# Weight tiles converted in pairs inside their load slots, with the order of the work tuned anew, in a delta-rule attention followed by two MLPs

## The chip, the cores and the metric

One core of a Trainium2 chip runs the whole program. The metric is the device time of one execution in microseconds (us), lower is better; where several runs are shown, their median counts.

## The reference

Four batches of eight heads go through a delta-rule recurrence over 768 tokens with head dimension 48, and its output, laid out as 3072 tokens by 384, goes through two MLPs without norms:

```python
k_n = k / (norm(k, axis=-1) + 1e-6)
for t in range(S):
    y[:, :, t] = einsum('bhd,bhde->bhe', q[:, :, t], state)
    v_old = einsum('bhde,bhd->bhe', state, kt)
    state = state + bt * einsum('bhd,bhe->bhde', kt, vt - v_old)
x = y.transpose(0, 2, 1, 3).reshape(3072, 384)
h = x @ w_in;   g = h * sigmoid(1.702 * h);   x = g @ w_out        # 384 -> 2048 -> 384
h = max(x @ moe2_w_in, 0);   out = (h * h) @ moe2_w_out
```

## The kernel before, in words

**Attention.** The 768 tokens are 12 chunks of 64. All 32 heads lie side by side, 16 pairs of them. For each chunk `run_a` makes the products k·k and k·q on TensorE (PE), `solve_in`, `solve_norm` and `solve_prep` make a triangular system out of them, `solve_loop` solves it by 31 steps of two small instructions each (chunks 0 and 1 by `solve_blocks`, 15 steps on half-size blocks, closed by `merge`), and the scan (`scale_v`, `run_x`, `finish`, `run_w`, `run_v`, `run_y`, `run_s`) makes the output y and the next state. The solves of chunks 2 to 11 run on GpSimd (POOL); that of chunk 1 goes where `TUNE["solve1"]` says, VectorE (DVE) here; that of chunk 0 is on DVE.

**MLPs.** A unit (`step`) is one tile of 128 hidden features for one group of tokens: 9 matmuls of the first layer into a PSUM bank `h`, an activation (ScalarE, ACT), and, two units later, 9 matmuls of the second layer (`layer2`) into three banks `z` that collect over all 16 tiles. Each product is three matmuls, of a high part and a low part of both sides (hi·hi, lo·hi, hi·lo). A group is 512 tokens, two chunks, with 16 units; there are six groups per MLP. The first group is cut: 8 units on the 256 tokens of chunk 0, 8 units on those of chunk 1, then 8 units on all 512, so units 0 to 23; the second group begins with unit 24 and needs the outputs of chunks 2 and 3. While group j is computed, the two chunks of group j + 1 are solved and scanned.

**Weights.** They arrive as 64-bit floats, 384 of them per partition and tile (384 KB). There are 64 tiles, 32 for each MLP (`wi`, `wo`; then `vi` and `wo` again). `load_w` (L375) loads one tile into one of three slots `raw`; `split_w` (L380) converts it with five instructions: on ACT the high word scaled into the buffer `c0`, on ACT (or DVE, in the second MLP, `tail`) the top three bits of the low word into one of two buffers `c1`, on DVE the two joined by shift and or into `c1` (L349), on ACT the high part `hi`, on DVE or POOL the low part `lo` = joined − hi (L342). The slot is free once the third instruction has run; `c1` is free after the fifth. `convert` (L1044) does that for n tiles and issues the next load after each. The z results of the first MLP go out through the same slots.

**Order.** Nothing is in program order: `Program.flush` is a list scheduler. It keeps one ready queue for each engine, takes the operation with the lowest rank that its cost figures say is ready, and writes the instructions of each engine in that order, which the chip then keeps. Rank is the place in the Python program, so the `TUNE` tables (L31) set it: `first` and `conv` say after which unit how many tiles are converted, `scan`, `solve`, `gscan`, `gsolve` at which unit each part of a chunk's scan and solve stands, `spread` does so for the weights of the second MLP, `holds` and `late` hold back loads behind a tiny DMA, `norm_pool` names the chunks whose norms go on POOL, `v_pool` and `lo_both` what may go on POOL or DVE, `p_late` when the k·q products are taken out of PSUM. `warm`, `burst`, `tiny`, `lead`, `fills`, `pad` and `auto` put idle matmuls on zeros (L306, L680, L1058, `tiny` L1061) between the real ones, which keep PE busy in the early part. Operations marked `urgent` go ahead of their rank (the solve of chunk 0 and, with `solve1='dve'`, that of chunk 1).

Of the kernel before, what the change touches and what calls it, by code (L numbers as in the profile page):

```python
# [19 lines left out]
C = 64  # L20
# [12 lines left out]
    warm=(0, 1, 0, 2, 0, 1, 1, 0, 1, 0, 1, 0, 0, 0, 1, 0),  # L33
    burst=(2, 7, 120),
    spread=1.85,
# [3 lines left out]
    slack=0.1,  # L39
# [20 lines left out]
    gscan=(0.0, 2.0, 2.0, 3.5, 3.5, 7.5),  # L60
    gsolve=(-9.0, -8.0, -2.5, -1.5),
    solve={2: (-8.0, -7.0, -5.5, -2.5), 3: (3.0, 8.0, 12.0, 12.5), 4: (14.5, 19.0, 21.0, 21.5), 5: (21.5, 24.1, 30.2, 31.5)},
# [164 lines left out]
def kernel(  # L227
# [54 lines left out]
    s_sb = att.tile([128, NP, D], F32, name="s_sb")  # L282
# [3 lines left out]
    q_sb = several(att, "q", 2, [128, NP, C])  # L286
# [5 lines left out]
    kT_sb = att.tile([128, 4, 4, C], F32, name="kT_sb")  # L292
# [81 lines left out]

    def load_w(src, f):  # L375
        s = n_conv[0] % NR
        n_conv[0] += 1
        dma(raw_sb[s], src[:, f].rearrange("p (n two) -> p n two", two=2), [], [("raw", s)], 128, 8 * DM)

    def split_w(key, f, hi, lo):  # L380
        s, t = n_conv[1] % NR, n_conv[1] % 2
        n_conv[1] += 1
        raw, c0, c1 = raw_sb[s], c0_sb[0], c1_sb[t]
        low = raw.rearrange("p n two -> p (n two)").bitcast(U16).rearrange("p (n q) -> p n q", q=4)[:, :, 1]
        both = [("c1", t)]
# [36 lines left out]
    V = [("v", g, k) for g in range(2) for k in range(2)]  # L422

# [548 lines left out]
    zs_of = [(("raw", i), t.rearrange("p n two -> p (n two)").bitcast(F32)[:, :TT]) for i, t in enumerate(raw_sb)]  # L972

    def layer2(ph, j, f, c0, n, hi, lo, K):
# [8 lines left out]
        if f == NF - 1:  # L983
            dst = zd if ph == 1 else out
            for e in range(KX):
                key, zs = zs_of[ns[1] % NR]
# [54 lines left out]
    w1 = [x for f in range(NF) for x in ((w1_in, "wi", f, wi_hi, wi_lo), (w1_out, "wo", f, wo_hi, wo_lo))]  # L1041
    w1_load = list(w1)

    def convert(todo, load, n, key=None):  # L1044
        for _ in range(n):
# [3 lines left out]
            if load:  # L1049
                load_w(*(load[0][0], load.pop(0)[2]))  # L1050

    with tc.manual_schedule():
# [66 lines left out]
        convert([], w1_load, NR)  # L1119
# [27 lines left out]
        convert(w1, w1_load, TUNE["first"])  # L1147
# [75 lines left out]
        zs_of[:] = [(("zs", i), t) for i, t in enumerate(several(p2, "zs", NR, [128, TT]))]  # L1223
# [8 lines left out]
        w2 = [x for f in range(NF) for x in ((w2_in, "vi", f, vi_hi, vi_lo), (w2_out, "wo", f, wo_hi, wo_lo))]  # L1232
# [125 lines left out]
```

## Time and profile before

| | us |
|---|---|
| three runs | 971.37, 973.64, 976.02 (median 973.64) |
| the profiled execution | 970.17 |
| its span, first to last instruction | 968.4 |
| start of the units 0, 8, 16, 24 (first `h` matmul in the timeline) | 45.0, 94.2, 114.1, 167.2 |
| chunk 1, 2, 3 solved (transpose `Td<-U`) | 47.6, 114.6, 149.1 |

The profiled execution lies 3.5 us under the median. The span is what the trace shows; the other 1.8 us of the execution lie around it.

### The profile page before, as it was taken

How to read it: one execution, taken by the hardware profiler on the slowest of the kernel's cores; microseconds unless marked ns; L12 is line 12 of the kernel's file. 1: busy time of each engine (PE TensorE's matmuls, PEld its weight loads, DVE VectorE, ACT ScalarE, POOL GpSimd, SP SyncE). 2: the span in 40 equal slices, each digit the busy share in tenths (PEclk: the TensorE clock that was granted, in tenths of full speed). 3: DMA queues.
4: the chain of work that ended last, by engine and by line, in shares of the span. 5: the costliest groups of instructions: out<-in, count | busy, mean ns of one | idle time of the engine just before them, and what ended most of it. 6: DMA issues, size and time to landing. Idle time of an engine off the chain costs nothing.

```text
span 968.4 us, 25919 instructions
## 1 busy us (share of the span) xinstructions
PE 937.9 (97%) x11079; PEld 758.8 (78%) x11079; DVE 474.9 (49%) x943; ACT 455.0 (47%) x927; POOL 328.0 (34%) x700
## 2 busy tenths in 40 slices
PE   7788999999999999999999999999999999999998
PEld 4566877787687778778888888888888888888886
DVE  7767866724643672554325456643433433433332
ACT  5368786325624534452466465642332422422322
POOL 3158883885578388477700010000000000000000
PEclk9789999999999999999999999999999999999999
DMA  5466562304401330430025353220010100000000
GB/s 189 162 198 215 158 183 77 109 1 127 148 14 43 125 120 2 127 101 17 23 90 165 96 177 98 66 66 1 24 42 0 61 5 1 34 1 0 33 1 33
DMA packets 34633, 75.83 MB, mean 78 GB/s; under 512 B 6326, under 2 KB 7382, under 8 KB 34518
## 3 DMA queue, kind: packets, MB, share of 16 engines
q1 hardware_dynamic: 34518, 74.17, 24.6%
q8 instruction: 87, 1.43, 0.6%
q14 instruction: 28, 0.23, 0.1%
HBM read 63.64 MB, written 9.44 MB: 75 GB/s over the span
## 4 chain that ended last, share of the span: by engine, by line
PE 82%; DVE 5%; POOL 5%; ACT 3%; issue 3%; DMA 1%; SPq 0%; ACTq 0%; POOLq 0%; DVEq 0%
PE h L369 37%; PE z L369 36%; PE a L369 8%; POOL U L749 2%; POOL tmpp L745 2%; DMA xf_sb<-Td 1%; PE z L306 1%; DVE c L349 1%; ACT w_sb L331 1%; DVE glo L342 0%; DVE wo_lo L342 0%; DMA k_sb<-in_kt 0%; SPq L313 0%; ACT h L326 0%; ACT wi_hi L326 0%
## 5 line engine op out<-in xcount | busy, mean ns | idle before, releaser
L369 PE MATMUL z<-ghi,wo_hi 128*128 128x512 f32 (+1 forms) x600 | 231.4, 386 | 0.0
L369 PE MATMUL z<-glo,wo_hi 128*128 128x512 f32 (+1 forms) x600 | 229.6, 383 | 0.4 <-DVE glo L342 0.4
L369 PE MATMUL z<-ghi,wo_lo 128*128 128x512 f32 (+1 forms) x600 | 229.1, 382 | 0.0
L342 DVE TENSOR_TENSOR glo<-h,ghi 128x512 fp32r<-128x512 f32 (+1 forms) x200 | 133.4, 668 | 193.9 <-ACT ghi L326 192.8
L745 POOL TENSOR_TENSOR tmpp<-U,gu 128x126 f32<-128x126 f32 (+22 forms) x310 | 139.3, 449 | 60.9 <-DVE U L346 38.3
L342 DVE TENSOR_TENSOR h<-g_sb,h 128x512 f32<-128x512 f32 x96 | 66.8, 696 | 175.2 <-ACT g_sb L326 175.2
L326 ACT ACTIVATE ghi<-h 128x512 fp32r<-128x512 f32 (+1 forms) x200 | 115.7, 580 | 59.5 <-DVE h L342 56.2
L326 ACT ACTIVATE g_sb<-h 128x512 f32<-128x512 f32 x96 | 57.2, 596 | 173.4 <-PE h L369 172.6
L749 POOL TENSOR_TENSOR U<-U,tmpp 128x126 f32<-128x126 f32 (+22 forms) x310 | 129.8, 419 | 24.3
L369 PEld LDWEIGHTS z<-ghi,wo_hi 128*128 128x128 f32 x600 | 113.1, 189 | 23.5
L369 PEld LDWEIGHTS z<-glo,wo_hi 128*128 128x128 f32 x600 | 113.2, 189 | 23.1 <-DVE glo L342 1.1
L369 PEld LDWEIGHTS z<-ghi,wo_lo 128*128 128x128 f32 x600 | 113.2, 189 | 22.2 <-DVE wo_lo L342 0.2
L369 PE MATMUL h<-x_hi,wi_hi 128*128 128x512 f32 (+1 forms) x312 | 124.0, 398 | 4.2 <-DVE glo L342 3.2
L326 ACT ACTIVATE h<-h 128x512 f32<-128x512 f32 (+1 forms) x104 | 57.2, 551 | 145.2 <-PE h L369 144.8
L369 PE MATMUL h<-x_lo,wi_hi 128*128 128x512 f32 (+1 forms) x312 | 117.3, 376 | 1.4 <-issue 1.4
L369 PE MATMUL h<-x_hi,wi_lo 128*128 128x512 f32 (+1 forms) x312 | 117.2, 375 | 1.5 <-POOL wi_lo L342 0.8
L369 PE MATMUL h<-x_hi,vi_hi 128*128 128x512 f32 x288 | 112.0, 389 | 0.0
L369 PE MATMUL h<-x_hi,vi_lo 128*128 128x512 f32 x288 | 112.0, 389 | 0.0
L369 PEld LDWEIGHTS h<-x_hi,wi_hi 128*128 128x128 f32 x312 | 59.0, 189 | 20.0 <-DVE glo L342 4.9
L369 PEld LDWEIGHTS h<-x_hi,wi_lo 128*128 128x128 f32 x312 | 59.0, 189 | 13.8 <-issue 1.6
L369 PEld LDWEIGHTS h<-x_lo,wi_hi 128*128 128x128 f32 x312 | 59.1, 189 | 9.0 <-DVE x_lo L342 0.4
L369 PEld LDWEIGHTS h<-x_hi,vi_hi 128*128 128x128 f32 x288 | 54.0, 188 | 11.2
(153 smaller groups left out, 1156.9 us busy)
## 6 DMA issues: line engine op xcount, KB each, us to landing
raw<-in_w_in SPq DMA_DIRECT2D x32, 384.0 KB, 3.2
raw<-in_w_out SPq DMA_DIRECT2D x32, 384.0 KB, 3.9
kq<-in_kf SPq DMA_DIRECT2D x44, 256.0 KB, 3.5
kT_sb<-in_kq SPq DMA_DIRECT2D x11, 512.0 KB
q<-in_kq SPq DMA_DIRECT2D x11, 512.0 KB, 5.6
k_sb<-in_kt SPq DMA_DIRECT2D x12, 384.0 KB, 3.8
v_sb<-in_vt SPq DMA_DIRECT2D x12, 384.0 KB, 7.2
xf_sb<-zd SPq DMA_DIRECT2D x18, 256.0 KB, 3.1
```

What stands on the lines that cost most here:

```text
L306: e.matmul(out=z_ps[KX - 1][:, 0:w], lhsT=z0[:, 0:128], rhs=z0[:, 0:w], start=not z_open[0], stop=not z_open[0])
L326: pg.add("act", c_act(n, kw["out"].shape[0]), lambda e: e.activation(**kw), reads, writes, early)
L331: e.activation(out=out, in_=in_, func=AF.Copy)
L342: pg.add(queue, cost, lambda e: e.tensor_tensor(out=out, in0=in0, in1=in1, op=op), reads, writes, early)
L349: pg.add("dve", c_dve(n), lambda e: e.scalar_tensor_tensor(**kw), reads, writes, early)
L369: e.matmul(out=out, lhsT=lhsT, rhs=rhs, start=start, stop=stop)
L745: e.tensor_tensor(out=t, in0=U[:, c0 + lo:c0 + hi, w:w + 1].to_broadcast(shape), in1=gu[:, :w, w:w + 1].rearrange("p i o -> p o i").to_bro ...
L749: e.tensor_tensor(out=y, in0=y, in1=t, op=ALU.add)
```

## The change

A slot now holds two neighbouring tiles (768 KB), and there are two slots. All five instructions work on 768 elements instead of 384 and inside the slot: the high word is scaled in place, the top bits are written over the low word, the join is written over the high word, and `hi` and `lo` are made from there. `c0` and `c1` are gone. The slot is therefore free only after the fifth instruction. There is one conversion for each pair, 16 in each MLP, and `first`, `conv` and `spread` count pairs. The z results use thirds of the two slots. `tail` is on ACT in both MLPs. The code can also take spare buffers as slots (`extra`), but `NX = 0`. For that, two attention tiles are allocated as parts of larger ones, at the same size.

In the order of the work: the solve of chunk 1 goes to POOL and is no longer urgent; the norms of chunk 4 go to POOL; `scale_v` of chunk 2 may go to POOL; the loads of chunk 0's q stand behind those for chunk 1 (`q_first`); the first weight loads are no longer held behind the tiny DMA (`holds`); three pairs instead of three tiles are converted before unit 0 (`first`); the products k·q leave PSUM earlier (`p_late`); positions of scans and solves move by up to some units; and the idle matmuls are placed anew.

```diff
-    warm=(0, 1, 0, 2, 0, 1, 1, 0, 1, 0, 1, 0, 0, 0, 1, 0),
-    burst=(2, 7, 120),
-    spread=1.85,
+    warm=(0, 3, 0, 2, 3, 1, 0, 0, 1, 0, 1, 1, 3, 0, 3, 3),
+    burst=(0, 8, 80),
+    spread=1.0,
...
-    q_first=1,
+    q_first=0,
-    lead=0,
-    holds=(1, 1, 1),
-    late=8,
-    conv=(3, 1, 1, 4, 0, 1, 2, 0, 1, 0, 0, 0, 0, 3, 3, 1, 1, 4, 4, 1, 2, 1, 3, 0, 0, 4, 1, 1, 7, 0, 6, 6),
-    lo_both=99,
-    v_pool=2,
-    tiny=(0, 40),
+    lead=16,
+    holds=(1, 0, 1),
+    late=9,
+    conv=(0, 2, 0, 1, 1, 0, 0, 3, 0, 0, 0, 1, 0, 1, 3, 1, 1, 0, 0, 1, 0, 0, 1, 0, 3, 0, 0, 0, 0, 3, 1, 0),
+    lo_both=32,
+    v_pool=3,
+    tiny=(24, 224),
-    solve1='dve',
-    pad={27: 2, 147: 3, 36: 4, 33: 6, 217: 1, 48: 2, 28: 3, 20: 1, 41: 1, 12: 3},
-    auto=(3.0, 1.3, 290),
-    fills=(2, 0, 0, 0),
-    norm_pool=(1, 2),
-    tail=('act', 'both'),
+    solve1='pool',
...
+    auto=(4.5, 0.9, 110),
+    fills=(1, 0, 1, 13),
+    norm_pool=(1, 2, 4),
+    tail=('act', 'act'),
-    p_late=400,
-    scan={1: (-4.5, -4.5, -3.0, -2.5, -1.0, 1.0), 2: (11.5, 11.5, 11.5, 11.5, 12.5, 14.5), 3: (14.5, 19.0, 19.5, 19.5, 21.5, 22.0)},
+    p_late=50,
+    scan={1: (-9.5, -9.0, -8.0, -7.5, -4.5, -1.0), 2: (10.0, 11.0, 11.0, 13.0, 13.0, 15.0), 3: (17.5, 20.0, 20.0, 22.5, 22.5, 23.0)},
-    solve={2: (-8.0, -7.0, -5.5, -2.5), 3: (3.0, 8.0, 12.0, 12.5), 4: (14.5, 19.0, 21.0, 21.5), 5: (21.5, 24.1, 30.2, 31.5)},
+    solve={2: (-14.5, -10.5, -10.5, -6.0), 3: (7.0, 8.5, 12.5, 12.5), 4: (13.5, 19.0, 20.5, 21.5), 5: (23.0, 23.6, 29.7, 31.5)},
...
-    NR = 3
-    raw_sb = several(main, "raw", NR, [128, DM, 2], I32)
-    c0_sb = several(main, "c0", 1, [128, DM])
-    c1_sb = several(main, "c1", 2, [128, DM])
+    NR, PW = 2, 2
+    raw_sb = several(main, "raw", NR, [128, PW * DM, 2], I32)
...
     def split_w(key, f, hi, lo):
-        s, t = n_conv[1] % NR, n_conv[1] % 2
+        raw, K, (high, least_) = raw_of(n_conv[1])
         n_conv[1] += 1
-        raw, c0, c1 = raw_sb[s], c0_sb[0], c1_sb[t]
+        high, least_, n = [high], [least_], PW * DM
...
+        whole = raw[:, :, 1].bitcast(F32)
+        parts = whole.rearrange("p (f n) -> p f n", f=PW)
+        hi, lo = hi[:, f:f + PW, :], lo[:, f:f + PW, :]
...
-        act(DM, [("raw", s)], ["c0"], out=c0, in_=raw[:, :, 1].bitcast(F32), func=AF.Prelu, scale=2.0**-112, alpha=2.0**32)
...
-        pg.add(queue, cost, tail, [("raw", s)], both)
-        stt(DM, ["c0"] + both, both, out=c1.bitcast(I32), in0=c0.bitcast(I32), scalar=3, in1=c1.bitcast(I32),
+        act(n, K + high, high, out=whole, in_=whole, func=AF.Prelu, scale=2.0**-112, alpha=2.0**32)
...
+        pg.add(queue, cost, tail, K + least_, least_)
+        stt(n, K + high + least_, high, out=raw[:, :, 1], in0=raw[:, :, 1], scalar=3, in1=raw[:, :, 0],
             op0=ALU.logical_shift_left, op1=ALU.bitwise_or)
-        act(DM, both, [(key, f, 0)], out=hi[:, f, :], in_=c1)
-        tt(DM, both + [(key, f, 0)], [(key, f, 1)], lo[:, f, :], c1, hi[:, f, :], ALU.subtract,
-           ("pool", "dve") if n_conv[1] <= TUNE["lo_both"] else "pool")
+        act(n, K + high, H, out=hi, in_=parts)
+        tt(n, K + high + H, L, lo, parts, hi, ALU.subtract, ("pool", "dve") if n_conv[1] <= TUNE["lo_both"] else "pool")
...
-            if load:
-                load_w(*(load[0][0], load.pop(0)[2]))
+            if load and n_conv[0] < NR + max(n_conv[1], NX):
+                load_w(load[0][0], load.pop(0)[2])
```

## Rows read from the trace of the kernel before

**Rows 1.** The page: busy time of each engine.
```profile
PE 937.9 (97%) x11079; PEld 758.8 (78%) x11079; DVE 474.9 (49%) x943; ACT 455.0 (47%) x927; POOL 328.0 (34%) x700
```

**Rows 2.** Busy time by stage; the row "core 0" names the columns.
```profile
core 0: us, PE busy (x) PEld busy (x) DVE busy (x) ACT busy (x) POOL busy (x), PEclk, DMA share, GB/s
27.00:45.00 18.00, 14.49 (x365) 9.71 (x365) 11.59 (x62) 4.94 (x14) 0.00 (x0) 0.66 0.50 171
45.00:69.00 24.00, 20.19 (x653) 16.74 (x647) 17.51 (x37) 15.41 (x39) 12.77 (x26) 0.86 0.67 201
69.00:94.00 25.00, 19.80 (x472) 16.36 (x471) 16.95 (x29) 21.21 (x54) 19.92 (x40) 1.00 0.60 192
...
149.00:167.00 18.00, 17.48 (x555) 13.77 (x553) 11.42 (x29) 11.59 (x27) 4.33 (x10) 1.00 0.25 69
...
508.00:640.00 132.00, 132.00 (x584) 109.32 (x583) 74.37 (x134) 78.33 (x155) 7.51 (x7) 1.00 0.40 117
```

**Rows 3.** The chain of waits, pieces in order of time: start, length, what.
```profile
149.10 1.10 DVE Td L759
...
167.22 1.92 PE h L369 x7
...
254.25 2.81 DMA xf_sb<-Td
```

**Rows 4.** Timeline of POOL: start, length, line, operation, out<-in, count, [idle before].
```profile
45.35 1.48 POOL L342 TENSOR_TENSOR w_sb<-v_sb,nt 128x768 f32<-128x768 f32 x1 [19.11 <-PE a L369]
...
52.27 2.35 POOL L543 TENSOR_SCALAR_AFFINE_SELECT p<-p 64x1024 f32<-64x1024 f32 x2 [1.06 <-ACT p L331]
54.70 0.24 POOL L564 TENSOR_SCALAR sm_y<-gu 128x32 int32<-128x32 int32 x1
...
62.49 0.25 POOL L568 TENSOR_TENSOR sm_a<-sm_b,sm_nu 128x32 f32<-128x32 f32 x1
...
69.40 0.49 POOL L745 TENSOR_TENSOR tmpp<-U,gu 128x31 f32<-128x31 f32 x1 [0.59 <-DVE U L346]
```

**Rows 5.** Groups by shape: count, then busy us, mean ns, idle before.
```profile
L326 ACT ACTIVATE ghi<-h 128x512 fp32r<-128x512 f32 x184 | 109.8, 598 | 59.3 <-DVE h L342 56.2
...
L349 DVE SCALAR_TENSOR_TENSOR c<-c,c 128x384 int32<-128x384 int32 x64 | 39.4, 615 | 4.2 <-ACT c L326 3.6 <-ACT c L389 0.3
...
L326 ACT ACTIVATE wo_hi<-c 128x384 fp32r<-128x384 f32 x32 | 16.8, 524 | 8.6 <-DVE c L349 7.8
```

**Rows 6.** Instructions on the tile wi_lo: min/median/max ns, first and last start.
```profile
L342 DVE TENSOR_TENSOR wi_lo<-c,wi_hi x11: 543/559/848, 61.0 to 144.9; 128x384 fp32r<-128x384 f32 x11
...
L342 POOL TENSOR_TENSOR wi_lo<-c,wi_hi x5: 992/1005/1020, 22.9 to 140.0; 128x384 fp32r<-128x384 f32 x5
```

**Rows 7.** Timeline of ACT: conversions, first and last G of chunk 2.
```profile
46.85 0.39 ACT L331 ACTIVATE G<-a 128x256 f32<-128x256 f32 x1 [0.27 <-PE a L369]
...
48.19 0.54 ACT L326 ACTIVATE c<-raw 128x384 f32<-128x384 f32 x1
...
51.52 0.40 ACT L331 ACTIVATE G<-a 128x256 f32<-128x256 f32 x1
...
82.82 0.56 ACT L326 ACTIVATE c<-raw 128x384 f32<-128x384 f32 x1
```

**Rows 8.** Timeline of DVE: chunk 1's solve, first and last; chunk 2's system; one `lo`.
```profile
28.14 0.67 DVE L705 SCALAR_TENSOR_TENSOR U<-gu,U 128x15 f32<-128x15 f32 x4
...
45.10 0.29 DVE L708 TENSOR_TENSOR gu<-U,gu 128x14 f32<-128x14 f32 x2
45.31 1.55 DVE L710 TENSOR_TENSOR U<-U,gu 128x14 f32<-128x14 f32 x2
...
66.72 1.23 DVE L342 TENSOR_TENSOR gu<-gu,sm_s 128x1024 f32<-128x1024 f32 x1
...
88.02 0.85 DVE L342 TENSOR_TENSOR wi_lo<-c,wi_hi 128x384 fp32r<-128x384 f32 x1
```

**Rows 9.** The page: one load of a weight tile, KB and median us to landing.
```profile
raw<-in_w_in SPq DMA_DIRECT2D x32, 384.0 KB, 3.2
```

More of the change, by code (lines that the diff above doesn't have):

```diff
@@ L281 @@
     w_sb = att.tile([128, NP, D], F32, name="w_sb")
-    s_sb = att.tile([128, NP, D], F32, name="s_sb")
+    ks_sb = att.tile([128, 16 * C + NP * D], F32, name="ks_sb")
+    kT_sb = ks_sb[:, 0:16 * C].rearrange("p (g a t) -> p g a t", g=4, a=4)
+    s_sb = ks_sb[:, 16 * C:].rearrange("p (a d) -> p a d", d=D)
     kq1_sb = several(att, "kq1", 2, [128, 2, 4, C])
@@ L285 @@
     p_sb = several(att, "p", 2, [128, NP, C])
-    q_sb = several(att, "q", 2, [128, NP, C])
+    q2 = att.tile([128, 2, NP, C], F32, name="q2")
+    q_sb = [q2[:, i] for i in range(2)]
     G_sb = several(att, "G", 2, [128, NP, C])
@@ L373, with raw_of @@
     n_conv = [0, 0]
+    def raw_of(n):
+        own = [("half", n % (NX + NR), i) for i in range(2)]
+        if n < NX:
+            t, keys = extra[n]
+            return t.bitcast(I32).rearrange("p (m two) -> p m two", two=2), keys, own
+        s = (n - NX) % NR
+        return raw_sb[s], [("raw", s, i) for i in range(3)], own
     def load_w(src, f):
-        s = n_conv[0] % NR
+        raw, keys, own = raw_of(n_conv[0])
         n_conv[0] += 1
-        dma(raw_sb[s], src[:, f].rearrange("p (n two) -> p n two", two=2), [], [("raw", s)], 128, 8 * DM)
+        dma(raw, src[:, f:f + PW].rearrange("p f (n two) -> p (f n) two", two=2), [], keys + own, 128, 8 * DM * PW)
@@ L387, in tail @@
+        hi, lo = hi[:, f:f + PW, :], lo[:, f:f + PW, :]
+        H, L = ([(key, f + i, x) for i in range(PW)] for x in range(2))
         def tail(e):
             if e is nc.scalar:
-                e.activation(out=c1.bitcast(I32), in_=low, func=AF.Copy, scale=7.499 / 65535)
+                e.activation(out=raw[:, :, 0], in_=low, func=AF.Copy, scale=7.499 / 65535)
             else:
-                e.tensor_scalar(out=c1.bitcast(I32), in0=raw[:, :, 0], scalar1=29, scalar2=None, op0=ALU.logical_shift_right)
@@ L393, in split_w @@
-        act(DM, [("raw", s)], ["c0"], out=c0, in_=raw[:, :, 1].bitcast(F32), func=AF.Prelu, scale=2.0**-112, alpha=2.0**32)
-        queue, cost = {"dve": ("dve", 0.38), "act": ("act", 0.42), "both": (("dve", "act"), (0.38, 0.42))}[TUNE["tail"][n_conv[1] > 32]]
-        pg.add(queue, cost, tail, [("raw", s)], both)
-        stt(DM, ["c0"] + both, both, out=c1.bitcast(I32), in0=c0.bitcast(I32), scalar=3, in1=c1.bitcast(I32),
+                e.tensor_scalar(out=raw[:, :, 0], in0=raw[:, :, 0], scalar1=29, scalar2=None, op0=ALU.logical_shift_right)
@@ L422 @@
     V = [("v", g, k) for g in range(2) for k in range(2)]
+    extra = [(q2.rearrange("p i a t -> p (i a t)")[:, 0:2 * DM * PW], [("q", 0), ("q", 1)]),
+             (ks_sb[:, 0:2 * DM * PW], KT + [("S", g) for g in range(2)])]
+    NX = 0
     def load_tok(n):
@@ L971 @@
     prev = []
-    zs_of = [(("raw", i), t.rearrange("p n two -> p (n two)").bitcast(F32)[:, :TT]) for i, t in enumerate(raw_sb)]
+    zs_of = [(("raw", i % NR, i // NR), raw_sb[i % NR].rearrange("p n two -> p (n two)").bitcast(F32)[:, TT * (i // NR):TT * (i // NR + 1)]) for i in range(3)]
     def layer2(ph, j, f, c0, n, hi, lo, K):
@@ L985, in layer2 @@
             for e in range(KX):
[L986 removed]
+                key, zs = zs_of[ns[1] % 3]
                 ns[1] += 1
@@ L1038, in step @@
             layer2(*prev.pop(0))
-    w1 = [x for f in range(NF) for x in ((w1_in, "wi", f, wi_hi, wi_lo), (w1_out, "wo", f, wo_hi, wo_lo))]
+    w1 = [x for f in range(0, NF, PW) for x in ((w1_in, "wi", f, wi_hi, wi_lo), (w1_out, "wo", f, wo_hi, wo_lo))]
     w1_load = list(w1)
@@ L1118 @@
             hold(1, p_sb[n - 1][0:1, 0, 0:1], [("P", 0, n - 1, 0)])
-        convert([], w1_load, NR)
+        convert([], w1_load, NX + NR)
         pg.gate = ()
@@ L1146 @@
         pg.gate = ()
-        convert(w1, w1_load, TUNE["first"])
+        convert(w1, w1_load, max(NX, TUNE["first"]))
         run_s(0)
@@ L1222 @@
         w_in_of[2] = (vi_hi, vi_lo)
-        zs_of[:] = [(("zs", i), t) for i, t in enumerate(several(p2, "zs", NR, [128, TT]))]
+        zs_of[:] = [(("zs", i), t) for i, t in enumerate(several(p2, "zs", 3, [128, TT]))]
         x_hi.append(p2.tile([128, KX, TT], F32R, name="x_hi1"))
@@ L1230, in load_z @@
                 dma(xf_sb[:, c], zd[128 * c:128 * c + 128, TT * j:TT * j + TT], [("zd", j, c)], xf_keys(c, 0, TT), 128, 4 * TT)
-        w2 = [x for f in range(NF) for x in ((w2_in, "vi", f, vi_hi, vi_lo), (w2_out, "wo", f, wo_hi, wo_lo))]
+        w2 = [x for f in range(0, NF, PW) for x in ((w2_in, "vi", f, vi_hi, vi_lo), (w2_out, "wo", f, wo_hi, wo_lo))]
         w2_load = list(w2)
```

12 lines of the change are left out of this document (6 added, 6 removed).

## The prediction

> **What bounds it now.** I read the page first: PE is busy for 97% of the span, every other engine for half of it or less [rows 1]. A change that only makes ACT, DVE and POOL cheaper can thus gain only where PE waits, so the next view is busy time by stage [rows 2]. From 508 to 640 us, where the second MLP's weights are converted, PE is busy 132.0 of 132.0 us; nothing can be gained there. From 27 to 45, 45 to 69 and 69 to 94 us PE is idle for 3.5, 3.8 and 5.2 us, its granted clock is 0.66 of full speed in the first of these stretches and 0.86 in the second (between its levels of 1.2 and 2.4 GHz), and part of the busy time is idle matmuls. The reader is to see that all that can be won lies ahead of unit 24.
>
> The chain of waits says what unit 24 waits for [rows 3]: the transpose after chunk 3's solve stands at 149.10, the first matmul of unit 24 at 167.22, and between them lies chunk 3's scan. Chunk 3 is solved on POOL right after chunk 2, so POOL's timeline is next [rows 4]: chunk 2's loop begins at 69.40. From there to 149.10 two solves take 79.7 us, while PE has only the first group's units and three chunks to do. After unit 24 PE is nearly always busy, with one wait left that the chain shows, the DMA at 254.25 ahead of the third group [rows 3]. So the question is how early chunk 2's loop starts, and whether weights, PE and POOL follow.
>
> **Part 1, the pairs.** A 128x384 conversion on ACT takes 524 ns, a 128x512 operation 598 [rows 5]: (598 − 524) / 128 = 0.58 ns an element. A pair of 768 is then 524 + 384 × 0.58 = 746 ns instead of 2 × 524, about 0.3 us less for each of three instructions; over 16 pairs 0.3 × 3 × 16 = 14 us of ACT before unit 24. Profiled lengths overlap at their ends, so 14 is the upper bound and 0 the lower; I take 7, half. DVE's `lo` (0.559 [rows 6]) lies between 0.56 and 1.12 for a pair; DVE's 128x1024 multiply takes 1.23 [rows 8], and on the line between the two 768 takes 0.96. The join (0.615 mean [rows 5]) is costed the same: 2 × 0.16 × 16 = 5 us of DVE less in all. No time of these is on PE's path by itself: it counts only where it delays chunk 2's system, below. In the second MLP it is 0: PE has no gap there, with ACT busy 78.33 and DVE 74.37 of 132 us [rows 2]; moving the last top-bit instructions from DVE to ACT leaves both under 70%. If that cover were gone it would cost what the conversions cost, and none of them is due sooner than some ten units later.
>
> **Part 2, the early stage.** Chunk 1's solve leaves DVE. There it ran from 28.14 to 47 [rows 8], because it shared DVE with chunk 0's scan; on POOL it is 30 instructions of 0.24 to 0.49 us [rows 4], 0.33 taken, plus gaps of some 0.1, 13 us, so it ends near 41, and POOL is idle then (0.00 of 18 us [rows 2]). DVE and ACT are free to convert: ACT is busy 4.94 of 18 us, and the third tile's high words are scaled at 48.19 only [rows 2, 7]. Afterwards three or four pairs, six to eight tiles, can be ready at 48 instead of two. The loads stand: two slots of 768 KB replace three of 384, no longer behind the hold; q of chunk 0 moves behind four loads of 256 KB on SP, under a microsecond of issue each, and is first used some 25 us later. I cost these moves at 0, bounds −1 to +1.
>
> What this gives chunk 2: its four G copies on ACT run from 46.85 to 51.52 [rows 7], 4.7 us for 4 × 0.4, since conversions stand between; about 2 us go. POOL's norms begin at 54.70 after 2.35 us of masks of chunk 1 [rows 4], which may come earlier; 0 to 2, taken as 0. The norms end at 62.7 and DVE's multiply starts at 66.72 [rows 4, 8], 4.0 us, in which DVE has three instructions of the norms' size (0.24 to 0.25 [rows 4]) to do; conversions ready earlier take 2 to 3 of that away. Sum: the loop starts 4 to 5 us sooner, I take 5 with ACT's savings of part 1. In the solves, `lo` instructions on POOL (1.0 us each [rows 6]) become half as many and up to twice as long: 0.
>
> Chunk 0's own scan is no longer interleaved with a solve, and idle matmuls are put anew where the clock is 0.66 and 0.86. At full clock these two stretches would lose nothing of 18 × 0.34 + 24 × 0.14 = 9.5 us; a filler that stands ahead of a real matmul costs its own time. Bounds −6 to +6; I take −2, a third of the first stretch's loss, because the chain there alternates PE with ACT and DVE.
>
> **Part 3, later.** Chunk 4's norms go to POOL: 20 instructions, from 54.70 to 62.74 for chunk 2's [rows 4], 8 us. POOL is busy only 4.33 of 18 us between the solves of chunks 3 and 4 [rows 2], so they fit there, and DVE is relieved; 0, bounds −2.8 (the wait for 254.25's DMA, 2.81 long [rows 3], goes whole) to +6 (they delay chunk 5's solve and that wait grows). The other positions only break ties of rank; bounds −3 to +3, taken as 0.
>
> **Sum.** −5 − 2 = −7 us. The profiled execution goes from 970.17 to 963.2; the runs' median, 973.64, stands 3.5 us above it, and from it the prediction is 966.6 us.
>
> **Against the change.** While POOL's 128x768 operation ran, from 45.35 for 1.48 us [rows 4], a DVE pair that took 0.29 us just before took 1.55, until that operation's end [rows 8]. So a DVE instruction can be held for the rest of a POOL one. The change puts 13 us of POOL work beside chunk 0's scan and makes each `lo` on POOL between 1.5 us (that row) and 2.0 (twice 1.0 [rows 6]) long. Most DVE instructions of that scan read PSUM, so I count nothing for it in the sum and make it a rival.
>
> The Trainium skill (SBUF — State Buffer, section SBUF: two separate sides) states that VectorE and GpSimd share one port pair as an exclusive lock, which whoever starts first keeps for the whole instruction. The trace agrees for this pair of rows; by that rule without exception the sum would be about 0 instead of −7, the case of the first rival.
>
> **Rivals.**
> (a) *POOL holds DVE up.* Some ten DVE instructions of chunk 0's scan each wait up to 0.49 us [rows 4] for a POOL one, about 5 us, and some three `lo` pairs on POOL hold DVE for 0.8 us each longer than now, 2.4 us: +7 against −7, no change, 973.6. For it: rows 4 and 8. Against it: the `lo` at 88.02 takes 0.85 [rows 8], but DVE's median one 0.559 [rows 6], though POOL runs its loops beside nearly all of them.
> (b) *The slots, slower.* A slot is now held until `lo` has run. Now, from the scaled high word at 82.82 to the end of that tile's `lo` at 88.87 it is 6.1 us [rows 7, 8], 2.8 of them the five instructions' own and 3.3 queueing; a pair would need some 3 × 0.75 + 2 × 0.96 = 4.2 and the same queueing, 7.5, and its load lands in 3.2 (as one tile [rows 9]) to 6.4 us. A slot turns round in 10.7 to 13.9 us. Before, the third to the thirty-first tile were converted between 48.19 and 144.9 [rows 6, 7], 29 tiles in 96.7 us; as 14.5 pairs on two slots that is one turn in 13.3, and with three more pairs ready early in 16.8. Beyond that point weights become the wait, and behind them PE with all units queued in order. At 13.9 with nothing ready early and 2 us of queueing a turn, 14.5 × 15.9 / 2 = 115 us, 18.6 later than 96.7. Of the 22 us from 144.9 to unit 24, unit 23 with the second layers behind it and chunk 3's matmuls need about 10, so 12 are slack: +7, 980.6. For it: ACT is busy 21.21 of 25 us from 69 to 94 [rows 2], so queues are long. Against it: early pairs.
> (c) *Much faster.* Chunk 2's system could start when chunk 1's solve leaves POOL: 41 + 2.35 for the masks + 8 for the norms + 2 for the multiply is 54, 15 us ahead of 69.40. PE's 24 units would allow it. The G copies at 46.85 [rows 7], which hang on chunk 0's state, speak against it. −15 us: 958.6, with a better clock −20: 953.6.
> That the change does not do what it says is only possible in that POOL's `lo` and chunk 1's solve crowd each other; this is in (a).
>
> **Chances.** Forecast 0.50, (a) 0.14, (b) 0.24, (c) 0.12. 0.5%, 4.9 us, is about what a measurement of this kernel can tell from no change. Of the forecast 0.40 lies beyond 4.9 us and 0.10 within; with (c) faster is 0.52. (a) and 0.03 of (b) lie within: 0.27. Slower 0.21. The range reaches down to (c) with its better clock, 953, and up to 979, just under (b)'s price, since a milder turn costs less; the unknown clock (±6) and positions (±3) around 966.6 lie inside.
>
> **What the profile would show.** Right: the joins and `lo` at 128x768 near 0.95 us, ACT's near 0.75; 30 POOL instructions on chunk 1's solve between 27 and 45; three or more pairs converted by 48; chunk 2's loop starting about 62 to 65; unit 24 about 160; PE without gaps from 508 to 640. Wrong: the loop starting at 69 or later (a); loads of `raw` issued only after a `lo` while PE waits for `wi_lo` or `wo_lo` (b); the loop near 54 (c); or a new wait ahead of the third group, then chunk 4's norms are to blame.

## The result, and the profile after

The changed kernel takes 980.28 us (median of 5 runs, 979.59 to 983.22) beside 972.18 us of the kernel before (5 runs on the same chip): ratio 1.0082 [1.0055, 1.0109], 8 us slower. The forecast was 966.6. The profiled execution took 980.00 us with a span of 978.3.

The page after, first the busy time of each engine, then the loads of the weights (KB each, median us to landing):

```profile
PE 949.1 (97%) x11198; PEld 766.9 (78%) x11198; DVE 449.8 (46%) x798; ACT 456.6 (47%) x850; POOL 343.9 (35%) x743
...
raw<-in_w_in SPq DMA_DIRECT2D x16, 768.0 KB, 4.4
raw<-in_w_out SPq DMA_DIRECT2D x16, 768.0 KB, 5.0
```

DVE has 25.1 us less to do than before [rows 1], ACT no less, and PE is as full as it was: shares over the whole span show nothing of the loss. The stages do. Busy time by stage after, with the columns of [rows 2]:

```profile
27.00:45.00 18.00, 12.73 (x278) 7.24 (x277) 6.13 (x14) 5.24 (x13) 13.06 (x32) 0.76 0.74 257
45.00:69.00 24.00, 21.41 (x635) 17.96 (x634) 14.70 (x21) 14.35 (x30) 12.22 (x26) 0.95 0.50 158
69.00:94.00 25.00, 24.38 (x633) 21.61 (x632) 13.39 (x21) 21.14 (x42) 17.52 (x31) 0.91 0.50 163
508.00:600.00 92.00, 86.70 (x376) 69.75 (x376) 50.29 (x60) 68.31 (x102) 5.93 (x3) 1.00 0.49 157
508.00:640.00 132.00, 126.70 (x552) 102.90 (x552) 63.65 (x80) 80.05 (x121) 5.93 (x3) 1.00 0.34 110
```

From 508 to 640 us PE was busy for 132.00 of 132 [rows 2] and is now idle for 5.3, all of it before 600, while ACT (80.05) and DVE (63.65) have ample time left. A measure that does not depend on where a stage begins is the time from the last `z` result of group 4 to that of group 6, counted through both MLPs (the two groups beside which the second MLP's weights are converted): 512.10 to 642.33 = 130.23 us before, 514.69 to 652.06 = **137.37 us** after. That is +7.1 of the 9.8 us between the two profiled executions. Nearly all the rest, 2.6, stands ahead of it: unit 24 starts at 172.1 instead of 167.2, and by group 4 half of that is made up. The profiled execution of before also lay 2.0 us under its median, so next to nothing of the 8 us is left for the early part.

What PE waits for there (the waits from 508 to 640: us in total, times, longest):

```profile
DVE raw L349 <- ACT raw L400: 22.6, 14, 3.9
...
PEld h L369 <- DVE glo L342: 7.1, 5, 3.1
ACT raw L326 <- DMA raw<-in_w_in: 6.9, 4, 3.3
...
PE h L369 <- DVE glo L342: 5.0, 4, 2.7
```

PE waits for `glo`, the low part of an activation, not for a weight; its weight loads (PEld), which stand ahead of its matmuls, wait 7.1 us for it, as much as the stage lost. ACT waits for a load. The chain of waits from 510 to 600 joins the two; one turn of it, start and length:

```profile
540.21 0.90 ACT raw L326
541.10 0.77 ACT raw L400
...
542.99 0.81 ACT vi_hi L326
543.82 0.97 DVE vi_lo L342
544.81 4.40 DMA raw<-in_w_in
549.23 0.90 ACT raw L326
```

It is a closed loop: the slot's load lands, ACT scales and takes the top bits, DVE joins, ACT makes `hi`, DVE makes `lo`, which frees the slot, and the next load starts, 4.4 us. ACT's timeline shows its period and who pays for it (in brackets the idle time before, and what ended it):

```profile
531.18 0.88 ACT L326 ACTIVATE raw<-raw 128x768 f32<-128x768 f32 x1 [3.26 <-DMA raw<-in_w_in]
531.97 0.89 ACT L400 ACTIVATE raw<-raw 128x768 int32<-128x768 uint16 x1
532.76 0.57 ACT L326 ACTIVATE h<-h 128x512 f32<-128x512 f32 x1
...
540.21 0.90 ACT L326 ACTIVATE raw<-raw 128x768 f32<-128x768 f32 x1 [1.84 <-DMA raw<-in_w_in]
...
549.23 0.90 ACT L326 ACTIVATE raw<-raw 128x768 f32<-128x768 f32 x1 [1.14 <-DMA raw<-in_w_in]
...
558.18 0.89 ACT L326 ACTIVATE raw<-raw 128x768 f32<-128x768 f32 x1 [0.68 <-DMA raw<-in_w_in]
```

The first slot's turns start at 531.18, 540.21, 549.23 and 558.18: **9.0 us a turn**. With `spread=1.0` a turn of both slots (one pair of `vi`, one of `wo`) falls due every two units, and two units last 8.1 us of PE (130.2 us for 32 units before; the expectations below round it to 8.2). So each of these turns comes some 0.9 us late. Over the eight turns of the 16 pairs that is of the size of the loss, but no more than that is shown: the turn before these took 12.3 us, the three after them 9.5 to 9.9, and the loss comes in a few waits of up to 3.1 us. ACT, which runs its written order, stands before the late load while the activation of a unit (`h` at 532.76) stands behind it.

### The profile page after: what moved, and what is told of

It is laid out like the page before. It is cut to its first block, busy times and chain, and to the rows that moved or that the text cites. A ratio compares the mean times of both kernels' runs of the same rounds, so it can differ in the third digit from the quotient of the medians.

```text
span 978.3 us, 25911 instructions
## 1 busy us (share of the span) xinstructions
PE 949.1 (97%) x11198; PEld 766.9 (78%) x11198; DVE 449.8 (46%) x798; ACT 456.6 (47%) x850; POOL 343.9 (35%) x743
## 4 chain that ended last, share of the span: by engine, by line
PE 84%; DMA 4%; ACT 4%; POOL 3%; issue 2%; DVE 2%; SPq 0%; ACTq 0%; DVEq 0%
PE h L369 37%; PE z L369 36%; PE a L369 9%; DMA raw<-in_w_in 2%; PE z L306 2%; POOL U L763 1%; POOL tmpp L759 1%; DMA raw<-in_w_out 1%; ACT raw L400 1%; ACT raw L326 1%; DMA kq<-in_kf 0%; ACT ghi L326 0%; ACT h L326 0%; DMA xf_sb<-Td 0%; ACT xf_sb L326 0%
## 5 line engine op out<-in xcount | busy, mean ns | idle before, releaser
L759 POOL TENSOR_TENSOR tmpp<-U,gu 128x126 f32<-128x126 f32 (+22 forms) x310 | 140.0, 452 | 57.2 <-DVE U L346 34.6
L763 POOL TENSOR_TENSOR U<-U,tmpp 128x126 f32<-128x126 f32 (+22 forms) x310 | 130.4, 421 | 24.3
```

What stands on the lines that cost most here:

```text
L759: e.tensor_tensor(out=t, in0=U[:, c0 + lo:c0 + hi, w:w + 1].to_broadcast(shape), in1=gu[:, :w, w:w + 1].rearrange("p i o -> p o i").to_bro ...
L763: e.tensor_tensor(out=y, in0=y, in1=t, op=ALU.add)
```

## The experiments

**Pace, in both kernels.** First the pace at which the second MLP's pairs fall due, put back in the new kernel, and put on the old one.

```diff
-    spread=1.0,
+    spread=1.85,
```

> The changed kernel with spread=1.85 instead of 1.0, nothing else: the weights of the second MLP are converted at the old pace, one pair of each kind in 3.7 units instead of 2; every instruction up to about 500 us is the same. Theory A (the turn of a slot: load, five instructions and the next load take 9.0 us for the two slots, but two units last 8.2 us, and ACT stands in order behind loads that have not landed, so that the units' own activations come late): with 15 us for each turn the wait is gone; PE is busy without a gap from 508 to 640 us, the z results of the groups that end at 581.5 and 649.3 come 6 to 7 us earlier, total 973 to 974. Rival B (the instructions of 0.9 us as such stand in the way of the units' activations, whatever the pace): the same number of them still falls in the way, 2 us or less is won. Rival C (what is lost comes from the early stage and only shows here): nothing is won.

Measured: 972.71 us (10 runs), ratio 1.0004 [0.9985, 1.0024]. The two groups take 130.2 us. One number of the change was worth all of the loss.

The same number in the kernel before:

```diff
-    spread=1.85,
+    spread=1.0,
```

> The kernel before with spread=1.0 instead of 1.85, nothing else: single tiles, three slots that are free after the third instruction, buffers between, but the pace of the changed kernel in the second MLP, two tiles a unit. Theory A (the long turn of the double slots is what PE waits for): these slots turn round three tiles in about 6 us and bear two tiles in 4.1 us, so there is no more than 1 us of loss, 972 to 973. Rival D (the pace alone crowds ACT and DVE, whatever the slots): 5 to 8 us are lost between 500 and 600 us, 977 to 980.

Measured: 971.83 us, 0.9996 [0.9977, 1.0014], 130.2 us for the two groups. Its stage row from 508 to 600 has PE full, with DVE busier (58.87 us) than in the kernel after (50.29) and ACT about as busy (66.19 and 68.31):

```profile
508.00:600.00 92.00, 92.00 (x407) 76.17 (x407) 58.87 (x110) 66.19 (x135) 7.59 (x7) 1.00 0.54 163
```

So the pace is harmless with three single slots that are free after the third instruction, and costs 7.1 us with two double ones that are held through the fifth. Neither half does it alone.

**The slots, the order, the size.** Three ways to break the loop at the fast pace. A third double slot for the second MLP only:

```diff
+        raw_sb.append(p2.tile([128, PW * DM, 2], I32, name="raw2"))
+        NR = 3
```

> The changed kernel, spread still 1.0, with a third double slot from the second MLP on (the memory of the attention stage is free by then); everything up to about 500 us is the same. Theory A (two slots cannot turn round fast enough for the pace): three slots have 12.3 us for a turn that takes about 9, so loads land before ACT is to use them, PE's waits from 508 to 600 us fall from 5.3 us to 1 or less, total 972.5 to 974. Rival B (instructions of 0.9 us at two pairs in two units are too much for ACT and DVE whatever the slots, ACT being busy 68 of 92 us there): 4 us or more are still lost, 977 to 980.

Measured: 975.23 us, 1.0030 [1.0016, 1.0043]; the two groups take 131.4 us. By the median some 3 us are left, more than the 1.2 of this stage; where the others lie is open. PE's idle time from 508 to 600 falls from 5.3 to 0.9 us with ACT as busy as in the kernel after (68.99 and 68.31):

```profile
508.00:600.00 92.00, 91.13 (x399) 74.16 (x398) 51.73 (x60) 68.99 (x104) 11.29 (x6) 1.00 0.45 153
```

The order alone, by telling the planner that a load lands later than it assumed, so that it places conversions behind the units' activations:

```diff
         pg.flush()
+        pg.DMA_END = 2.0
```

> The changed kernel, spread still 1.0, but the planner counts 2.0 instead of 0.5 us for the end of each load after the first flush (about 500 us on); only the order of the instructions changes. Theory A1 (the loss is made by order: ACT is told to scale a high word before the load has landed, and the unit's activation stands behind it): the planner now puts the activations first, the conversions come later, which no unit feels for ten units, and PE waits for 2 us at most instead of 7; 973 to 975. Rival A2 (the turn itself bounds, whatever the order): the same loss, 980, or more.

Measured: 973.76 us, 1.0024 [1.0008, 1.0040]; 130.9 us. The slots turn no faster (the first slot's turns take 9.0 to 12.7 us), but next to nothing that PE needs stands behind a load that has not landed:

```profile
508.00:600.00 92.00, 92.00 (x404) 75.35 (x403) 51.79 (x64) 68.33 (x103) 3.76 (x2) 1.00 0.47 155
```

So it is the order around the slow turn that costs, not the slow turn by itself.

Single tiles in four slots, still in place and held through `lo`:

```diff
-    first=3,
+    first=8,
...
-    NR, PW = 2, 2
+    NR, PW = 4, 1
```

with `conv` doubled entry by entry and `lo_both=64`.

> The changed kernel with PW=1 and NR=4: the same bytes of slots and conversion in place, but one tile in a slot and four slots, instructions on 384 elements; first=8 and conv doubled so that as many tiles are converted after each unit (two more before unit 0), lo_both doubled. Theory A (a turn is made of the load and of five instructions in a row): a single tile's load lands in 3.2 us and its instructions are half as long, so a turn is some 6.5 to 7 us for four tiles against 8.2 us for two units: the loss from 500 to 600 us is 2 us or less instead of 7. Rival E (holding the slot through the fifth instruction is what costs, at any size): 4 us or more are still lost there. The early stage is planned anew by this too, so the total can move by some 4 us either way from it; the verdict is read from the stage.

Measured: 980.71 us, 1.0091 [1.0065, 1.0117]. In the second MLP the loss is gone (131.1 us), as expected of the loop; but the early part is worse (unit 24 at 176.8, group 4's last `z` at 520.0 instead of 514.7), because positions found for pairs were simply doubled. As a time it says nothing on pairs against singles; as a stage it does.

**How sharp the threshold is.** By the loop, a pace of 1.2 should have been enough (2 × 1.2 units, 9.8 us, against 9.0).

```diff
-    spread=1.0,
+    spread=1.2,
```

> The kernel after with spread=1.2: in the second MLP the conversion of a pair falls due every 2.4 units, 1.2 times further apart than in the kernel after. Theory A (a closed loop: load, conversion and freeing of a slot take 9.0 us a turn of two pairs, and the loss is the turn's excess over the time that the pace gives): two units last 8.2 us, by the pace of 1.2 a pair is due every 9.8 us, above the 9.0 us that the loop takes for a pair's slot, so that PE has next to no gap: the two groups behind the eviction of group 4 take 130.3 to 131.5 us (137.4 at 1.0, 130.3 at 1.85), and the median is 972.5 to 974.5. Rival P (the loss falls in proportion as the pace slows, because each conversion costs PE something): 1.2 is about a quarter of the way from 1.0 to 1.85, so the two groups take 135 to 136 us and the median is 977 to 979.

Measured: 975.84 us, 1.0043 [1.0017, 1.0070]; the two groups take 134.6 us. Both theories missed, A by much, P narrowly in the stage and by more in the time. ACT's timeline:

```profile
538.39 0.89 ACT L326 ACTIVATE raw<-raw 128x768 f32<-128x768 f32 x1 [1.67 <-DMA raw<-in_w_in]
...
547.21 0.90 ACT L326 ACTIVATE raw<-raw 128x768 f32<-128x768 f32 x1
...
556.02 0.90 ACT L326 ACTIVATE raw<-raw 128x768 f32<-128x768 f32 x1
...
564.98 0.90 ACT L326 ACTIVATE raw<-raw 128x768 f32<-128x768 f32 x1 [0.49 <-DMA raw<-in_w_in]
```

The first slot's turns shown are still 8.8 to 9.0 us apart, so the loop is what sets them. My 9.8 was a mean: the code rounds due times down to whole units, 1, 3, 6, 8, 10, 13, 15, 18, so that four of the seven steps are still two units, 8.1 us, shorter than a turn. Four sevenths of 7.1 us are 4.1, beside the 4.4 measured. This fit was made afterwards and is not shown to be the cause: the slot turns at 8.8 to 9.0 us also where its step is three units, since its first turn takes 12.3 us here as in the kernel after, and the next ones may only catch that up.

**The early part: pairs without their positions.** The new conversion with the whole table of the kernel before (`conv` and `first` counted in pairs, `lo_both=32`):

```diff
-    spread=1.0,
+    spread=1.85,
...
-    holds=(1, 0, 1),
+    holds=(1, 1, 1),
...
-    solve1='pool',
+    solve1='dve',
...
-    norm_pool=(1, 2, 4),
+    norm_pool=(1, 2),
...
-    scan={1: (-9.5, -9.0, -8.0, -7.5, -4.5, -1.0), 2: (10.0, 11.0, 11.0, 13.0, 13.0, 15.0), 3: (17.5, 20.0, 20.0, 22.5, 22.5, 23.0)},
+    scan={1: (-4.5, -4.5, -3.0, -2.5, -1.0, 1.0), 2: (11.5, 11.5, 11.5, 11.5, 12.5, 14.5), 3: (14.5, 19.0, 19.5, 19.5, 21.5, 22.0)},
```

> Only the conversion is changed: pairs in place in two double slots, but every tuning value of the kernel before, with conv counted in pairs so that as many tiles are converted after each unit (first=3 pairs), spread=1.85. It tells what the pairs alone do. Theory J (the wider instructions save ACT and DVE little and hold POOL's solve on the shared path: a POOL instruction of the solve that runs beside a 128x768 DVE one takes 1.0 to 1.2 us instead of 0.5): chunk 2's and 3's solves take 3 to 6 us longer together than the 79.7 us before, total 973 to 979. Rival K (the forecast: fewer and cheaper conversions make the early stage faster): unit 24 at 162 us or earlier, total 966 to 969.

Measured: 977.63 us, 1.0060 [1.0037, 1.0083]; no loss in the second MLP (130.4 us). Chunk 2's loop starts at 68.8 as before, but that solve and the next take 84.1 us for 79.7, and unit 24 starts at 172.2. So the pairs alone cost about 5 us in the early part, and the new table (972.71 at the slow pace) wins about 5 back. The retuning is no gain on top of the pairs; it repairs them. It does so behind unit 24, not ahead of it: the five profiles that run the early part in the order of the kernel after (its own and those of the runs at 1.85, at 1.2, with the third slot and with the later landing) start unit 24 at 171.5 to 176.0, no earlier than this run, and take 341.4 to 342.6 us from there to the last `z` of group 4, where this run takes 347.1 and the kernel before 344.9.

**What the pairs cost there.** The traces offered a suspect: in the solve of chunk 2 GpSimd has 15 instructions over 0.75 us in the kernel after and 4 before. POOL's timeline after, then DVE's in the same stretch:

```profile
89.49 0.51 POOL L759 TENSOR_TENSOR tmpp<-U,gu 128x133 f32<-128x133 f32 x1
90.08 1.25 POOL L763 TENSOR_TENSOR U<-U,tmpp 128x133 f32<-128x133 f32 x1
91.41 1.09 POOL L759 TENSOR_TENSOR tmpp<-U,gu 128x126 f32<-128x126 f32 x1
92.57 1.03 POOL L763 TENSOR_TENSOR U<-U,tmpp 128x126 f32<-128x126 f32 x1
93.68 1.11 POOL L759 TENSOR_TENSOR tmpp<-U,gu 128x136 f32<-128x136 f32 x1
```

```profile
90.06 2.09 DVE L349 SCALAR_TENSOR_TENSOR raw<-raw 128x768 int32<-128x768 int32 x2
92.23 1.08 DVE L342 TENSOR_TENSOR wo_lo<-raw,wo_hi 128x768 fp32r<-128x768 f32 x1
93.23 1.19 DVE L342 TENSOR_TENSOR wi_lo<-raw,wi_hi 128x768 fp32r<-128x768 f32 x1
```

While DVE's wide instructions run, POOL's 0.5 us instructions take 1.0 to 1.25, and the last three of these end (92.57 + 1.03 is 93.60) 0.3 to 0.4 us after one of DVE's (93.31 for that one). To test whether time hangs on it, each of these two DVE instructions was cut in two at its place in the order, in the new kernel at the slow pace and in the run with the old table.

```diff
-        stt(n, K + high + least_, high, out=raw[:, :, 1], in0=raw[:, :, 1], scalar=3, in1=raw[:, :, 0],
-            op0=ALU.logical_shift_left, op1=ALU.bitwise_or)
+        def join(e):
+            for i in range(PW):
+                r = slice(i * DM, (i + 1) * DM)
+                e.scalar_tensor_tensor(out=raw[:, r, 1], in0=raw[:, r, 1], scalar=3, in1=raw[:, r, 0],
+                                       op0=ALU.logical_shift_left, op1=ALU.bitwise_or)
...
+                for i in range(PW):
+                    e.tensor_tensor(out=lo[:, i], in0=parts[:, i], in1=hi[:, i], op=ALU.subtract)
```

> The kernel after with spread=1.85, and the two instructions that a pair needs on VectorE (the join and the low part) each given as two of 384 elements, one behind the other, in the same place of the same order. Theory M (in the early part the 0.96 us instructions hold GpSimd's solves, whose short instructions wait until one ends): of the solve of chunk 2, the instructions over 0.75 us fall from 15 to 6 or fewer, their sum from 36.8 to about 33 us, unit 24 starts 2 to 4 us earlier, and the median is 969 to 971 us beside 972.7 of the slow-pace kernel. Rival N (VectorE holds GpSimd for the same total time, however it is cut, since two halves come back to back; or the chain of chunk 2 is set by its order and not by these holds): the sum stays at 36 us or more or the sum falls and unit 24 does not move, and the median stays within 1.5 us of 972.7, or rises by what 20 more instructions cost.

> The pair conversion with the whole tuning of the kernel before (as in the run that gave 977.6 us), and the join and the low part on VectorE each cut in two instructions of 384 elements in the same place of the order. Theory M (what the pairs cost in the early part is the width of their instructions on VectorE, which hold GpSimd's solves): the solve of chunk 2 has 5 or fewer instructions over 0.75 us for 12, and the sum falls from 34.2 towards the 32.2 us of the kernel before; unit 24 starts at 167 to 169 us for 172.2, and the median is 972.5 to 974.5. Rival N (the width on VectorE does not matter; the pairs cost the early part by their length on ScalarE, their later freeing of slots and the order that these set): unit 24 stays at 171 to 173 and the median within 1 us of 977.6.

Measured: 972.06 us, 0.9999 [0.9975, 1.0023], and 976.56 us, 1.0049 [1.0024, 1.0074]. POOL's timeline of the first, where the four long instructions are 0.85, 0.69, 0.64 and 0.70 now, and one row of later:

```profile
90.08 0.85 POOL L776 TENSOR_TENSOR U<-U,tmpp 128x133 f32<-128x133 f32 x1
91.01 0.69 POOL L772 TENSOR_TENSOR tmpp<-U,gu 128x126 f32<-128x126 f32 x1
91.78 0.64 POOL L776 TENSOR_TENSOR U<-U,tmpp 128x126 f32<-128x126 f32 x1
92.49 0.70 POOL L772 TENSOR_TENSOR tmpp<-U,gu 128x136 f32<-128x136 f32 x1
...
114.70 0.62 POOL L772 TENSOR_TENSOR tmpp<-U,gu 128x31 f32<-128x31 f32 x1 [3.26 <-DVE U L346]
```

The holds go just as theory M says: 15 long instructions become 2 and their sum over the solve falls from 36.8 to 33.1 us (70 instructions in both, the first steps of the next solve among them); with the old table 12 become 1, 34.2 to 30.2 (68 in both). But from the loop's start to chunk 2's transpose it is 51.4 us for 51.0, and 49.5 for 49.4. Rival N is right on the time: the 3.7 us freed are spent waiting, most of them in the row at 114.70, the first step of chunk 3's solve, which stands within chunk 2's in POOL's order and waits for DVE. The holds are real and cost nothing by themselves.

Last, POOL freed of all else: low parts of the first MLP on DVE alone, and the scale of chunk 2 back on DVE, on top of the halves at the slow pace.

```diff
-    v_pool=3,
+    v_pool=2,
...
-        both = n_conv[1] <= TUNE["lo_both"]
-        pg.add(("pool", "dve") if both else "pool", (c_pool(n), c_dve(n)) if both else c_pool(n), least_part, K + high + H, L)
+        both = n_conv[1] > NF * 2 // PW
+        pg.add(("pool", "dve") if both else "dve", (c_pool(n), c_dve(n)) if both else c_dve(n), least_part, K + high + H, L)
```

> The kernel of the run before (slow pace, VectorE's two wide instructions cut in halves), with the low parts of the first MLP on VectorE alone and the scale of chunk 2 back on VectorE, so that GpSimd does nothing beside the solves of the early chunks but masks and norms. Theory Q (GpSimd's own extra work stands in the chain: within the 51.4 us of chunk 2's solve, one low part with the wait for ScalarE ahead of it is 3.9 us and the scale with its wait 3.2; in the solve of chunk 1 two low parts are some 4): the solve of chunk 2 takes 44 to 46 us, unit 24 starts at 163 to 168 for 171.5, and the median is 964 to 969, faster than the kernel before. Rival R (GpSimd's solves wait for something else in the same places, as they did where the holds were taken away, or VectorE, with four more wide instructions ahead of the solve's own DVE steps, is late): the solve stays at 49 us or more and the median stays within 1.5 us of 972.1, or the solve shortens and unit 24 does not.

Measured: 973.75 us, 1.0008 [0.9994, 1.0023]. POOL now runs chunk 2's loop in 38.5 us (73.8 to 112.3) for 51.4, some 7 of which had gone to those first steps of chunk 3 and their wait. Chunk 2's transpose comes 44.1 us after the loop's start, as theory Q had it, 5.7 us behind POOL's last step, because DVE has other work ahead of it. But unit 24 starts at 177.0 for 171.5: rival R, its second form. The chain of waits from 60 to 178 has no POOL among its longest pieces any more (from 27 to 172 of the kernel after POOL's two loop instructions held 18.7%), but this:

```profile
91.22 0.94 ACT wo_hi L326
...
93.84 6.75 DMA raw<-in_w_out
100.61 0.94 ACT raw L326
101.55 0.80 ACT raw L400
102.37 1.28 DVE raw L410 x2
```

A load of weights of 6.75 us, its conversion, and PE's units behind that. So with 13 us taken off POOL the chain goes through a slot; that the slots, and not DVE's added work, are what bounds the time now is read from this chain alone and was not tried.

**Two moves that failed.** With the slow pace, chunk 1's solve back on DVE:

```diff
-    solve1='pool',
+    solve1='dve',
```

> The changed kernel with spread=1.85 (so that the second MLP's stage is out of the comparison) and chunk 1's solve back on DVE, urgent again; nothing else. It asks what moving that solve to POOL brought. Theory F (the move brought what was forecast: DVE and ACT free from 27 to 45 us, chunk 2's system earlier): without it chunk 2's loop on POOL starts later by 5 us or more, and the total is 976 to 979. Rival G (the move brought nothing, since the solved chunk 1 then waits on DVE behind chunk 2's transposes until 57 us): the transpose after chunk 1's solve comes by 50 us, chunk 2's loop starts within 2 us of the 71 to 75 us with the solve on POOL, total 970 to 974 against 972.7.

Measured: 978.79 us (6 runs, 975.17 to 985.47), 1.0079 [1.0049, 1.0108]. The solve moved as one theory has it, the time as the other. Chunk 2's loop starts at 69.0 and its solve is done at 112.8; in the five profiles with the solve on POOL and all else in the same order these stand at 70.8 to 75.1 and 121.5 to 126.1. Yet chunk 3's transpose stands at 159.2 for 154.6 to 159.0 and unit 24 at 176.5 for 171.5 to 176.0. The 9 to 13 us at chunk 2 are gone by chunk 3. The positions were found with the solve on POOL, so this is no verdict on where chunk 1's solve belongs.

And chunk 1's scan brought forward, since its transpose waits behind chunk 2's in DVE's order (the profile after):

```profile
55.17 2.07 DVE L352 STREAM_TRANSPOSE gu<-G 128x1024 f32<-128x1024 f32 x1 [1.97 <-ACT G L331]
57.18 1.00 DVE L773 STREAM_TRANSPOSE Td<-U 128x512 f32<-128x512 f32 x1
```

```diff
-    scan={1: (-9.5, -9.0, -8.0, -7.5, -4.5, -1.0),
+    scan={1: (-15.0, -9.0, -8.0, -7.5, -4.5, -1.0),
```

> The changed kernel with spread=1.85 and one position changed: the first part of chunk 1's scan (v scaled, state product, transpose of the solve) ranks ahead of chunk 2's products instead of behind its transposes. Theory H (chunk 1, solved at 45 us, is held until 57 us by rank alone, and this keeps the early stage from its gain): the transpose comes at 46 to 50 us, unit 8 starts 4 to 8 us earlier than 94.7 to 99; the total falls only as far as chunk 3's solve on POOL does, 0 to 4 us, 969 to 973. Rival I (POOL's chain is delayed by it, because chunk 2's products now come later): chunk 2's loop starts 2 us or more later, and the total is 974 to 977.

Measured: 996.83 us, 1.0253 [1.0224, 1.0283]. Chunk 1's transpose stands at 57.9 (56.8 to 61.1 in the five profiles without the move), chunk 2's loop starts at 91.2 (70.8 to 75.1), unit 24 at 189.0 (171.5 to 176.0). Both theories missed by far; one position moved a whole solve by 16 us or more. Why the planner put chunk 2's system so late was not looked into.

## Why the prediction was wrong, point by point

**Part 1, the pairs.** The lengths were nearly right: DVE's pair 0.96 us forecast, 0.959 measured; ACT's 0.746 forecast, while three in a row start 0.79 apart (531.18, 531.97, 532.76) and a single one takes 0.90. The rows on the tile `raw` from 500 to 620 (min/median/max ns):

```profile
L326 ACT ACTIVATE raw<-raw x16: 883/901/943, 518.9 to 592.6; 128x768 f32<-128x768 f32 x16
...
L349 DVE SCALAR_TENSOR_TENSOR raw<-raw x16: 944/959/961, 520.6 to 594.3; 128x768 int32<-128x768 int32 x16
```

**The step that failed** is "In the second MLP it is 0 ... none of them is due sooner than some ten units later". It was read from busy time (ACT and DVE under 70%, PE without a gap) and from when a weight is *needed*. What decides is when the *slot* is needed again: load, five instructions and queueing, twice over on two slots, in 8.1 us, with 9.0 measured. The spare time of ACT is no cover when its order is written: it stood idle ahead of the load, with the unit's activation behind it. The step was worth 0 in the sum and 7.1 us on the chip, undone by the pace (130.2 us for the two groups), and all but 0.7 to 1.2 us of it by the order or by a third slot, each alone.

The Trainium skill (Perfetto Trace Analysis, section Optimizing Scalar/DVE Operations) states that larger operations can help if the engine is saturated, and that where it isn't, but makes bubbles on others, breaking instructions up may let work finish sooner. The second MLP's rows agree as far as single tiles in four slots go (131.1 us for 137.4), a run that changes the loads and the count of slots too; wide instructions with a third slot lose as little (131.4), and the halves in the early part change nothing.

**Part 2, the early stage.** Forecast −5 and −2. At the slow pace the kernel as a whole equals the one before (1.0004), but the early stage itself is slower: unit 24 starts at 171.5 to 176.0 in the five profiles with this order, beside 167.2 in the kernel before and 168.5 in its run at the fast pace. By the last `z` of group 4 the difference is all but gone (513.0 to 517.5 us, beside 512.1 and 514.9); what wins it back stands in Part 3. By its steps: chunk 1's solve ends on POOL at 45.5, not 41, since a low part of 1.84 us and its wait, and masks, stand in it; 2 pairs are ready by 48, not 3 or 4; its transpose comes only at 57.2, behind chunk 2's transpose of `G`; chunk 2's loop starts at 71.2, not 62 to 65. The clock did rise (0.76 and 0.95 for 0.66 and 0.86 [rows 2]), as forecast, and fell to 0.91 from 69 to 94. The step "In the solves, `lo` instructions on POOL become half as many and up to twice as long: 0" was judged too lightly: with the old table, the three within chunk 2's solve cost 6.5 us for 3.7 before. Whether the 5 us that the pairs cost early come from these, from waits for ACT's `hi`, or from the slots was not separated; that most of them do not come from DVE's holds was shown (976.56 us with the halves for 977.63).

**Part 3.** Chunk 4's norms and the other positions stood at 0, with bounds that allow a gain. The stages show one: behind unit 24 the new table wins 2.3 to 3.5 us on the kernel before (341.4 to 342.6 us to the last `z` of group 4, for 344.9). PE's idle time from 167 to 508 is 4.1 us before, 1.9 after, and 7.8 in the run with the pairs and the old table, in this order:

```profile
167.00:508.00 341.00, 336.90 (x5522) 268.55 (x5515) 165.13 (x322) 156.42 (x323) 225.57 (x511) 1.00 0.24 76
167.00:508.00 341.00, 339.08 (x5646) 270.35 (x5646) 162.25 (x320) 158.80 (x329) 226.61 (x514) 1.00 0.25 78
167.00:508.00 341.00, 333.23 (x5610) 265.03 (x5611) 162.59 (x319) 154.87 (x322) 226.62 (x516) 0.99 0.22 70
```

Which of the new positions does it was not tried alone.

**Rival (a)**, POOL holding DVE, saw one direction of two. The kernel after has it: at 63.46 a low part on DVE took 2.53 us instead of 0.96, beside one of 1.87 that POOL had begun at 63.31. The rows above show DVE's wide instructions holding POOL as well, and taking those holds away brought no time; nor did the run without POOL's low parts, which changed more than this. The rule of the Trainium skill (SBUF — State Buffer, section SBUF: two separate sides), that the pair of ports is locked by whichever starts first for its whole instruction, fits both directions here.

**Rival (b)**, the slots, named the mechanism and, with 980.6, nearly the time; but it was placed in the first MLP, where its deciding point was 13.3 to 16.8 us a turn, and the loss came in the second, where it was 8.1. The agreement of the number is chance. With the turn that (b) itself estimated, 10.7 to 13.9 us, a look at the period (two units, 8.1) would have put it there: the diff's `spread=1.0` was read as a position and not as a period.

**Rival (c)** never began: the loop would have had to start near 54.

## What to carry to other kernels

When buffers become fewer, or are held longer, compute the turn (load, every instruction until the release, queueing) and compare it with the period at which the program wants them, stage by stage and step by step, since a mean period above the turn (9.8 for 9.0 us) still lost 4.4 us here; busy shares say nothing of it. In an engine with a written order, one instruction that waits for a load makes everything behind it late, so a slow turn of a buffer that nobody needs yet can still stop TensorE: give it a slower pace, one more slot, or a later place. And when one resource is freed by 4 or 13 us and the time does not move, look for the next wait in the chain before tuning that resource further.

## What the runs showed of the hardware that was not expected

- VectorE and GpSimd held each other up in both directions: DVE's instructions of 0.96 us stretched POOL's from 0.5 to between 1.0 and 1.25 us, and with DVE's cut in halves the same ones took 0.64 to 0.85; one of POOL's of 1.87 stretched one of DVE's from 0.96 to 2.53.
- A low part of 128x768 took 0.96 us on DVE (median) and 1.84 to 2.15 on POOL.
- Two tiles in one load of 768 KB landed in 4.4 us (`w_in`) and 5.0 us (`w_out`), beside 3.2 [rows 9] and 3.9 (the page before) for one of 384 (medians): fewer us for each tile, but 1.1 to 1.2 more in each turn of a slot.
- The early part scatters: the kernel after and its runs at spread 1.85, at 1.2, with the third slot and with the later landing give each engine the same order up to the second MLP's weights, and their profiled executions start unit 24 at 172.1, 176.0, 171.5, 173.1 and 171.6. One profile of it does not decide on 4 us.
